# One transfer of weights and one of keys change places in GpSimd's order of issue

## The chip, the cores and the metric

The kernel runs on one core of one Trainium2 chip. The time is that of the device for one execution, in microseconds. A core has five engines that run side by side, each with its own order of instructions: TensorE (PE; PEld is its weight load), VectorE (DVE), ScalarE (ACT), GpSimd (POOL) and SyncE (SP). Transfers between memory and the chip are issued by SyncE, GpSimd and, at the start, ScalarE, and are carried by 16 DMA engines. In the profile, q0 is the queue of transfers that GpSimd issues and q1 that of SyncE's.

## What is computed

Causal attention for 4 batches, 8 heads, 768 positions and head size 64, in which five of the heads see only 4 sink positions and a window of 64, followed by a gated feed-forward layer over the 3072 resulting rows:

```python
scores = q @ k^T / sqrt(64)                    # per batch and head
scores = where(mask, scores, -1e9)             # heads 0, 2, 6: causal; the others: causal and (sink or window)
x = softmax(scores) @ v                        # laid out as [3072, 512]
h = x @ w_in                                   # w_in  [512, 2048]
g = h * sigmoid(beta * h)
out = g @ w_out                                # w_out [2048, 512], out [3072, 512] f32
```

Inputs and output are float32; the kernel multiplies in bf16.

## The kernel before

The work is cut into eight chunks: a batch and a half of its positions (384 rows). They go two batches at a time, first halves ahead of second halves, so the third and fourth chunks (numbers 2 and 3) are the second halves of batches 0 and 1. A chunk has four units, each a pair of heads; unit 12 is the first of the fourth chunk. For a unit TensorE makes the scores (line 482), ScalarE their exponentials, VectorE or the added masks remove what is not seen, and TensorE multiplies with the values (line 563). For a chunk that is done, TensorE makes h in 16 groups (line 631), ScalarE and VectorE make g of it (lines 636 and 639), and TensorE makes three output tiles of 128 rows from the 16 pieces of g, in four parts of four products (line 684): the first part takes the first quarter of w_out, the fourth part the last. ScalarE copies an output tile out of its bank (line 688), and SyncE stores it (line 690).

Every engine's order is written out by hand. The string RAMP, a list of words that `do` carries out one by one, orders the first eight units; PLAN orders the rest, with `later` for steps that come due after a time of a planner's clock. The words that matter here:

- `wi0` to `wi3`: GpSimd issues one quarter of w_in (line 141); `wo0` to `wo3`: one quarter of w_out (line 145). Both turn float32 into bf16 on the way.
- `ro3`: GpSimd issues the next row load of the fourth chunk (`load_rows`, line 284). There are twelve: six of keys, then six of queries, each 128 rows of four heads, turned into bf16. They go into tile `s`.
- `dk3`, `dq3`: SyncE transposes the fourth chunk's keys into KT (line 300) and its queries into QTD (line 303), three transfers each; one needs two row loads.
- `vo1`, `vo2`, ...: GpSimd copies the values of a chunk's windows and sinks into VO (lines 261 and 262).

In the order of RAMP the transfers that GpSimd issues are, counted from one: the four of w_in (1 to 4), `wo0`, `wo1`, `wo2` (5 to 7), `ro3` (8), `wo3` (9), and the other eleven `ro3` (10 to 20), after which those of the fifth chunk follow. All wait their turn in one queue. Between them GpSimd has copies and casts to do, in its one order. `ro` and `wo` add nothing to the planner's clock.

The quarter of w_out is loaded, and a row load issued, by

```python
nc.gpsimd.dma_start(out=w_out_sb[:, f, :], in_=moe_w_out.rearrange("(fo fi) d -> fi fo d", fi=128)[:, f, :])
...
nc.gpsimd.dma_start(out=ROWS[c % 2, name][:, t, i * 4 * D:(i + 1) * 4 * D].rearrange("p (h d) -> p h d", d=D),
                    in_=src[b, i:H:2, r:r + 128, :].rearrange("h p d -> p h d"))
```

Of the kernel before, what the change touches and what calls it, by code (L numbers as in the profile page):

```python
# [18 lines left out]
def kernel(  # L19
# [792 lines left out]
    def feed(x):  # L812
# [20 lines left out]
        ex3.0 qk4.1 tk5 ad4.0 ex3.1 tq5 pv3 pv3 pv3 cx0a kk6v no2 qk4.0 tk7 ex4.1 kq5a kk5v no3 ko5 ex4.0 qk5.0 ko6  # L833
        kk7v wi1 tq6 xx1 ex5.0 ko7 qk5.1 ex5.1 tq7 kq6v ad6.0 kq7v cv1.0a cx1v wi2 qk6.0 wi3 ad6.1 ml1 qk6.1 ex6.0
        ex6.1 hm mm cv1.1g ma5.v mlg cv1.2g pv4 rk hf mm ad7.0 qk7.0 vo1 wo0 wo1 pv5 ma5.1 pv4 lq2.1g wo2 pv4 lv3.0g
        no4 ad7.1 qk7.1 lv3.1 ex7.0 pv5 rq pv7 pv5 pv6 pv7 no5 pv6 ro3 wo3 pv6 ex7.1 pv7 ml1 mm lv3.2 no7 no6 xx2
        ro3 cx2a mA mA xx3 ro3 cx3v mm mm mA mA mm mm ro3 mA mm mA mm mm mm mA cq8g mm mA mm ck8g mA mm mm mA mA mm
        ro3 mm mm ro3 mA mA mb mb tt8 mb mb mb
    """
# [114 lines left out]
```

## Time and profile before

| | us |
|---|---|
| median of 3 runs | 229.96 |
| the runs | 229.87 to 230.05 |
| the profiled execution | 230.6 |
| its span, first to last instruction | 228.9 |

The profile is of one execution. Its span is 1.7 us shorter than that execution's time. TensorE is busy for 97% of it, at a granted clock of 0.998 of full speed; ScalarE for 67%, VectorE for 61%, GpSimd for 38%. A row of the order of time gives start, duration, engine, line and operation, the tile written and the tile read, and in brackets the idle time ahead of it with what ended it. "DMA to landing" is the time from the start of the issuing instruction to the landing of its data.

### The profile page before, as it was taken

The numbers are of one execution on the slowest core, as the hardware profiler recorded it, in microseconds if no ns is written. First come the engines' busy times: TensorE is split into PE (matmuls) and PEld (weight loads), VectorE is DVE, ScalarE is ACT, GpSimd is POOL, SyncE is SP. The second block draws the span as 40 slices with busy tenths as digits, with TensorE's granted clock in tenths as the row PEclk, the third lists the DMA queues.
The fourth block names the chain that finished last, engine by engine and source line by source line (L and its number), as shares of the span: only waits on it lengthen the run. The fifth ranks groups of instructions, "written<-read, shape, count | busy, mean of one in ns | idle before, by whom it ended". The sixth has DMA issues, their size and how long they took to land.

```text
span 228.9 us, 5039 instructions
## 1 busy us (share of the span) xinstructions
PE 221.7 (97%) x1919; PEld 126.9 (55%) x1919; DVE 139.5 (61%) x343; ACT 153.6 (67%) x252; POOL 87.3 (38%) x144
## 2 busy tenths in 40 slices
PE   8999999979999999999999999999999999999993
PEld 3566666634555665555654565556645665456553
DVE  2578888852485679436942589566863779028600
ACT  2589788826867799348944797669876877138521
POOL 6467934168245369444039308960430000000000
PEclk9999999999999999999999999999999999999999
DMA  6999999999999799979779998799803030111012
GB/s 201 246 307 223 213 229 197 192 225 171 152 193 131 164 157 155 121 181 153 100 149 124 147 174 134 106 161 137 195 4 105 25 80 0 49 54 38 0 49 93
DMA packets 95384, 31.67 MB, mean 138 GB/s; under 512 B 81776, under 2 KB 92416, under 8 KB 95360
## 3 DMA queue, kind: packets, MB, share of 16 engines
q1 hardware_dynamic: 58880, 22.82, 49.2%
q0 software_dynamic: 35904, 8.13, 44.6%
q10 hardware_dynamic: 576, 0.40, 0.6%
q8 instruction: 15, 0.25, 0.5%
q14 instruction: 9, 0.07, 0.1%
HBM read 27.27 MB, written 6.29 MB: 147 GB/s over the span
## 4 chain that ended last, share of the span: by engine, by line
PE 76%; DMA 16%; POOL 3%; DVE 1%; ACT 1%; SPq 1%; issue 0%; ACTq 0%; POOLq 0%
PE mm L684 34%; PE mm L631 18%; DMA w_out_sb<-in_moe_w_out_dram 10%; PE sp L631 8%; PE sp L482 6%; PE po L563 6%; DMA vs<-in_v_dram 4%; DMA s<-in_q_dram 2%; PE mm L669 2%; POOL w_out_sb L145 1%; PE mm L353 1%; PE po L544 1%; PE mm L482 1%; DVE es L515 1%; POOL VX L253 1%; SPq L133 1%
## 5 line engine op out<-in xcount | busy, mean ns | idle before, releaser
L684 PE MATMUL mm<-w_out_sb,gT 128*128 128x512 bf16 x368 | 86.0, 379 | 1.4 <-DMA w_out_sb<-in_moe_w_out_dram 1.4
L491 ACT ACTIVATE es<-sp 128x768 bf16<-128x768 f32 (+2 forms) x72 | 56.5, 834 | 18.8 <-PE sp L482 18.5
L631 PEld LDWEIGHTS <-w_in_sb 128*128 128x128 bf16 x512 | 47.7, 98 | 30.1 <-issue 0.6
L631 PE MATMUL mm<-xT,w_in_sb 128*128 128x384 bf16 x340 | 63.3, 326 | 0.2 <-DVE gT L639 0.2
L684 PEld LDWEIGHTS <-gT 128*128 128x128 bf16 x368 | 33.4, 98 | 37.5 <-issue 3.1
L636 ACT ACTIVATE th<-mm,beta_h 128x384 f32<-128x384 f32 x85 | 48.4, 586 | 6.5 <-PE mm L631 1.8
L639 DVE SCALAR_TENSOR_TENSOR gT<-th,mm 128x384 bf16<-128x384 f32 x85 | 45.6, 550 | 7.1 <-ACT th L636 3.8
L631 PE MATMUL sp<-xT,w_in_sb 128*128 128x384 bf16 x172 | 33.6, 326 | 0.0
L688 ACT ACTIVATE osb<-mm 128x512 f32<-128x512 f32 x23 | 13.9, 602 | 27.1 <-PE mm L684 26.7
L563 PEld LDWEIGHTS <-es 128*128 128x128 bf16 x472 | 22.8, 98 | 11.9 <-issue 1.1
L253 POOL CAST VX<-vs 128x512 bf16<-128x512 f32 x15 | 9.5, 633 | 51.2 <-DMA vs<-in_v_dram 48.4
L639 DVE SCALAR_TENSOR_TENSOR gT<-th,sp 128x384 bf16<-128x384 f32 x43 | 23.3, 551 | 5.9 <-ACT th L636 3.7
L636 ACT ACTIVATE th<-sp,beta_h 128x384 f32<-128x384 f32 x43 | 24.8, 583 | 2.4 <-PE sp L631 0.2
L284 POOL DMA_DIRECT2D s<-in_k_dram x30 | 22.4, 758 | 9.4 <-DMA w_in_sb<-in_moe_w_in_dram 4.7
L563 PE MATMUL po<-VX,es 128*128 128x65 bf16 x360 | 24.7, 194 | 0.0
L284 POOL DMA_DIRECT2D s<-in_q_dram x30 | 22.5, 781 | 3.6 <-DMA w_out_sb<-in_moe_w_out_dram 2.7
L572 DVE RECIPROCAL rec<-po 128x6 f32<-128x6 f32 x28 | 5.4, 193 | 28.0 <-PE po L563 27.8
L482 PE MATMUL sp<-QTD,KT 64*128 64x128 bf16 (+2 forms) x258 | 19.2, 240 | 0.0
L509 DVE TENSOR_TENSOR es<-es,Mh 128x768 bf16<-128x768 bf16 (+1 forms) x26 | 14.8, 595 | 5.0 <-ACT es L491 4.4
L576 DVE TENSOR_TENSOR x<-po,rec 128x384 bf16<-128x384 f32 x28 | 15.6, 557 | 1.0
L482 PEld LDWEIGHTS <-KT 64*128 64x128 bf16 x278 | 11.0, 94 | 5.5 <-issue 3.7
L261 POOL COPY VO<-VX 128x512 bf16<-128x512 bf16 x16 | 10.0, 644 | 9.5 <-DVE VX L253 9.5
(75 smaller groups left out, 160.2 us busy)
## 6 DMA issues: line engine op xcount, KB each, us to landing
vs<-in_v_dram SPq DMA_DIRECT2D x24, 256.0 KB, 4.8
out_dram<-osb SPq DMA_DIRECT2D x23, 256.0 KB, 2.6
w_in_sb<-in_moe_w_in_dram POOLq DMA_DIRECT2D x4, 512.0 KB, 9.8
w_out_sb<-in_moe_w_out_dram POOLq DMA_DIRECT2D x4, 512.0 KB, 17.0
s<-in_k_dram POOLq DMA_DIRECT2D x30, 64.0 KB, 4.7
s<-in_q_dram POOLq DMA_DIRECT2D x30, 64.0 KB, 5.5
s<-in_k_dram SPq DMA_DIRECT2D x4, 384.0 KB, 8.7
s<-in_q_dram SPq DMA_DIRECT2D x4, 384.0 KB, 9.6
```

The costliest lines, as they stand in the source:

```text
L253: copy(out=VX[b % 2][:, h2 * HT + t, :, 0:D], in_=staged["v", c][:, t])
L284: nc.gpsimd.dma_start(out=ROWS[c % 2, name][:, t, i * 4 * D:(i + 1) * 4 * D].rearrange("p (h d) -> p h d", d=D), in_=src[b, i:H:2, r:r + 1 ...
L482: nc.tensor.matmul(sps[i][r][:, x * 128:y * 128], key(a, lhs), s["QT"][half(a), qi * 128:(qi + y - x) * 128], start=first, stop=first or y ...
L491: nc.scalar.activation(out=views[i].rearrange("p r k j -> p r (k j)"), in_=banks[2][:, :, 0:n * 128], func=ACTF.Exp, scale=scale)
L509: eng.tensor_mul(ev[:, :, 0:n], ev[:, :, 0:n], Mh[h2][:, None, m0:m0 + n].to_broadcast([128, 2, n, 128]))
L563: nc.tensor.matmul(po[:, qi, hh, :], e, val, start=(j == 0), stop=(j == len(lst) - 1))
L576: nc.vector.tensor_mul(xg[g][:, :, :, u % 2, :].rearrange("p a t d -> p t a d"), po[:, :, :, 0:D], rec.to_broadcast([128, HT, 2, D]))
L631: nc.tensor.matmul(hp[:, 0:HALF], w_in_sb[:, mo, fi * 128:(fi + 1) * 128], xT[c][:, mo, :], start=(mo == 0), stop=(mo == MO - 1))
L636: nc.scalar.activation(out=th, in_=hp[:, 0:HALF], func=ACTF.Tanh, scale=beta_h[:, fi:fi + 1])
L639: nc.vector.scalar_tensor_tensor(out=gTs[c][:, fi, :], in0=th, scalar=1.0, in1=hp[:, 0:HALF], op0=ALU.add, op1=ALU.mult)
L684: nc.tensor.matmul(op, gTs[c][:, fi, ns * 128:(ns + 1) * 128], w_out_sb[:, fi, :], start=(fi == 0), stop=(fi == FO - 1))
L688: nc.scalar.activation(out=osb, in_=op, func=ACTF.Copy, scale=0.5)
```

## The change

In RAMP the words `ro3 wo3` become `wo3 ro3`: GpSimd issues the last quarter of w_out as its eighth transfer and the fourth chunk's first row load of keys as its ninth. The other words, and all that the words do, stay as they are.

```diff
-        no4 ad7.1 qk7.1 lv3.1 ex7.0 pv5 rq pv7 pv5 pv6 pv7 no5 pv6 ro3 wo3 pv6 ex7.1 pv7 ml1 mm lv3.2 no7 no6 xx2
+        no4 ad7.1 qk7.1 lv3.1 ex7.0 pv5 rq pv7 pv5 pv6 pv7 no5 pv6 wo3 ro3 pv6 ex7.1 pv7 ml1 mm lv3.2 no7 no6 xx2
```

## The prediction

> **What bounds the kernel now.** I read the page first: the engines' busy time, then the chain that ended last, and then the order of time on TensorE and on GpSimd around the one place of that chain that is not TensorE's own work.
>
> ```profile
> span 228.9 us, 5039 instructions
> PE 221.7 (97%) x1919; PEld 126.9 (55%) x1919; DVE 139.5 (61%) x343; ACT 153.6 (67%) x252; POOL 87.3 (38%) x144
> ```
>
> TensorE has work for 221.7 of 228.9 us. A change pays, then, only where it shortens one of the few gaps on TensorE, or costs where it opens one. The chain of waits, from 28 us on, has this:
>
> ```profile
> 28.52 22.11 DMA w_out_sb<-in_moe_w_out_dram
> 50.67 3.61 PE mm L684 x16
> ```
>
> The chain runs through the transfer of w_out's last quarter: issued at 28.52, landed 22.11 us later, at 50.63, and the products of line 684 start 0.04 us behind it. After 50.67 the chain goes through TensorE, with a few stretches of ScalarE and VectorE, to the end. The order of time on TensorE shows how long it stood there:
>
> ```profile
> 48.28 1.03 PE L684 MATMUL mm<-w_out_sb,gT 128*128 128x512 bf16 x4
> 50.67 3.61 PE L684 MATMUL mm<-w_out_sb,gT 128*128 128x512 bf16 x16 [1.36 <-DMA w_out_sb<-in_moe_w_out_dram]
> ```
>
> The first twelve products of an output tile need quarters 0 to 2; the thirteenth needs quarter 3. TensorE was ready at 48.28 + 1.03 = 49.31 and idle for 1.36 us. This is the gap that the change bears on, and 1.36 us is the most that can be had from it directly.
>
> **What the change moves.** Two GpSimd instructions change places. The order of time on GpSimd (the idle time and its releaser stand in brackets):
>
> ```profile
> 27.02 0.76 POOL L145 DMA_DIRECT2D w_out_sb<-in_moe_w_out_dram  x1
> 27.79 0.77 POOL L284 DMA_DIRECT2D s<-in_k_dram  x1
> 28.52 0.78 POOL L145 DMA_DIRECT2D w_out_sb<-in_moe_w_out_dram  x1
> 29.25 0.79 POOL L284 DMA_DIRECT2D s<-in_k_dram  x1
> 31.59 0.74 POOL L284 DMA_DIRECT2D s<-in_k_dram  x1 [1.54 <-DMA w_in_sb<-in_moe_w_in_dram]
> ...
> 45.59 0.74 POOL L284 DMA_DIRECT2D s<-in_q_dram  x1 [2.66 <-DMA w_out_sb<-in_moe_w_out_dram]
> 46.93 0.74 POOL L284 DMA_DIRECT2D s<-in_q_dram  x1 [0.59 <-DMA s<-in_k_dram]
> 47.66 0.62 POOL L261 COPY VO<-VX 128x512 bf16<-128x512 bf16 x1
> 49.88 1.17 POOL L261 COPY VO<-VX 128x512 bf16<-128x512 bf16 x2 [1.59 <-DVE VX L253]
> 51.11 1.46 POOL L262 COPY VO<-VX 4x1536 bf16<-4x1536 bf16 x1
> 52.52 2.22 POOL L284 DMA_DIRECT2D s<-in_q_dram  x3
> 55.12 0.84 POOL L284 DMA_DIRECT2D s<-in_q_dram  x1 [0.37 <-DMA s<-in_k_dram]
> 56.41 0.74 POOL L284 DMA_DIRECT2D s<-in_k_dram  x1 [0.46 <-DMA s<-in_k_dram]
> ```
>
> The quarter's issue moves from 28.52 to 27.79, and the row load's from 27.79 to 28.57 (27.79 + 0.78). No instruction is added or taken away, and the 0.77 and 0.78 us of issue only trade places. The 0.73 us of earlier issue are not the gain: both transfers wait a long time in the queue behind others. What counts is where each stands in it, and for this I asked for single transfers' times from issue to landing (the last number of the pairs below; the first fence has the second and third quarters, of which the later, at 27.02, took 18.3).
>
> ```profile
> L145 POOL DMA_DIRECT2D w_out_sb<-in_moe_w_out_dram x2: 747/754/760, 26.2 to 27.0; - x2
> DMA to landing us min/median/max: 15.7/17.0/18.3
> ```
> ```profile
> L284 POOL DMA_DIRECT2D s<-in_k_dram x1: 770/770/770, 27.8 to 27.8; - x1
> DMA to landing us min/median/max: 18.9/18.9/18.9
> ```
> ```profile
> L145 POOL DMA_DIRECT2D w_out_sb<-in_moe_w_out_dram x1: 780/780/780, 28.5 to 28.5; - x1
> DMA to landing us min/median/max: 22.1/22.1/22.1
> ```
> ```profile
> L284 POOL DMA_DIRECT2D s<-in_k_dram x1: 790/790/790, 29.3 to 29.3; - x1
> DMA to landing us min/median/max: 23.1/23.1/23.1
> ```
>
> Issue plus duration gives the landings: third quarter 27.02 + 18.3 = 45.32; row load 27.79 + 18.9 = 46.69; last quarter 28.52 + 22.1 = 50.62; second row load 29.25 + 23.1 = 52.35. They land in the order of issue, 1.37, 3.93 and 1.73 us apart. So the GpSimd queue is being worked off in order and without a pause, and a row load holds it for about 1.4 to 1.7 us.
>
> **The sum.** Take the row load out from in front of the last quarter. The quarter then lands 3.93 us behind the third one, at 45.32 + 3.93 = 49.25, which is 1.37 us sooner. TensorE is ready at 49.31 and would find it there, or nearly: with the 0.04 us from landing to start of the chain, 49.29. The gap of 1.36 us goes to about 0. The bounds: a row load is worth nothing if it runs in the shadow of other transfers, and 1.73 us by the second row load's spacing, but the gap caps this at 1.36. So the direct gain lies between 0 and 1.36. I take 1.3, since the spacing of 1.37 was measured for this very transfer, at this very place, and a tenth may be lost where the two mixes of packets differ.
>
> Why should the row load have a cost of its own, at an eighth of the quarter's size (the page's list of issues: count, KB each, median us to landing)?
>
> ```profile
> w_out_sb<-in_moe_w_out_dram POOLq DMA_DIRECT2D x4, 512.0 KB, 17.0
> s<-in_k_dram POOLq DMA_DIRECT2D x30, 64.0 KB, 4.7
> ```
>
> The answer of the DMA view for 41.99 to 45.35 us, ahead of the third quarter's landing (queue, packets, MB, share of 16 engines):
>
> ```profile
> q1 hardware_dynamic: 819, 0.23, 47.6%
> q0 software_dynamic: 817, 0.40, 86.5%
> ```
>
> The GpSimd queue (q0) and SyncE's (q1) moved equally many packets, 817 and 819, though 0.40 against 0.23 MB: they take turns by packets, so a load of many small packets costs as many turns as one of large ones. The Trainium skill, "DMA: Bandwidth & Descriptors", section "Queues, rings and completion order", says that each engine goes round the queues that have work and changes over at packet borders; the counts here agree with it. By that rule the bytes of the load do not matter and its turns do. By bytes alone, 64 of 512 KB, the row load would be worth 3.93 / 8 = 0.49 us, and the gain with it.
>
> **What the swap does to others.** The first row load now comes behind the quarter. By the same spacings it lands where the quarter did, at about 50.6, and the second at 52.35 as before. The transposes of the fourth chunk's keys need both, so nothing is later for them.
>
> A wait changes its content, though. GpSimd's row loads at 31.59, 45.59 and 46.93 each wait for the transfer issued eight places earlier: 31.59 is the eleventh of the queue and waits for a piece of w_in, the third; 45.59, the fifteenth, starts 0.27 us behind the third quarter's landing (45.32), the seventh; 46.93, the sixteenth, 0.24 us behind the row load's (46.69), the eighth. With the change, the eighth is w_out's last quarter, landing at 49.25. So the row load of 46.93 starts at about 49.5, some 2.6 us later, and behind it in GpSimd's order stand the three copies of VO, line 262's copy and four more row loads. Counted on: issue to 50.2, the copies to 52.0 (0.62 + 1.17; their own wait on VectorE ended by 49.88), line 262 to 53.5, three row loads to 55.7 where they ended at 54.74, the next to 56.5, and the first row load of the chunk after at 56.5 instead of 56.41. The slip is 2.6 us at first, about 1 us behind the copies, and 0.1 us at the end, because the short waits that stood at 49.88, 55.12 and 56.41 take it up.
>
> Two covers hide it. One is the queue's backlog:
>
> ```profile
> L284 POOL DMA_DIRECT2D s<-in_q_dram x1: 740/740/740, 46.9 to 46.9; - x1
> DMA to landing us min/median/max: 11.8/11.8/11.8
> ```
> ```profile
> L284 POOL DMA_DIRECT2D s<-in_q_dram x1: 740/740/740, 52.5 to 52.5; - x1
> DMA to landing us min/median/max: 7.5/7.5/7.5
> ```
>
> The load of 46.93 landed at 58.7 and the next, issued at 52.5, at 60.0, right behind it. Issued at 49.5 and 53.5 they still have over 6 us of queue ahead of them. The other is the distance to who needs the result:
>
> ```profile
> 64.73 0.19 PE L563 MATMUL po<-VO,es 128*128 128x65 bf16 x1
> ```
> ```profile
> L303 SPq DMA_TRANSPOSE QTD<-s x1: 1190/1190/1190, 65.1 to 65.1; - x1
> DMA to landing us min/median/max: 3.2/3.2/3.2
> ```
> ```profile
> 71.73 0.61 PE L482 MATMUL sp<-QTD,KT 64*128 64x384 bf16 x8
> ```
>
> The VO copies end at 53.5, and the first product with VO comes at 64.73, or 63.4 if TensorE gains 1.3: ten us to spare. The fourth chunk's queries are transposed last at 65.1 and landed at 68.3; their first scores stand at 71.73, or 70.4 with the gain: 2.1 us to spare. This is the thinnest cover. If it were gone, each us of lateness would cost one.
>
> So the sum is -1.3 + 0 + 0. The profiled execution took 230.6 us with a span of 228.9, so it would be 229.3 with a span of 227.6. The median of the runs was 229.96, 0.64 below the profiled one; I take the same 1.3 off: 228.7.
>
> **Rivals.** First, no change: the last quarter lands at 50.6 wherever its issue stands, since the landing is that of the slowest of 16 engines and these were saturated. For it: the long 3.93 us spacing may be that of a straggling engine, which the row load's few packets would not have held up. Against it: the landings in order and the 1.37 us between third quarter and row load. The time would be 230.0. The Trainium skill, same page, "Two DMAs through the same engine are not ordered", says that nothing orders transfers across the 16 engines, which would speak for this; the four landings here came in order all the same. Chance 0.12.
>
> Second, slower: the changed wait. The sixteenth transfer now waits for a long one instead of a short one, and the queries behind it come late. It decides when the queries' last transposes land after 70.4 instead of 68.3, and it takes the whole gain once they land after 71.73, 3.4 us late. If the backlog hid none of it and the loads lost one more place, of a quarter's 3.93 us, the landing would be 72.2: a gap of 0.5 us over the old course, 230.5; with the 2.6 us of the wait on top, 74.8 and 233.1. For it: GpSimd's order is strict and the wait is sure to come. Against: the 6 us of backlog. Chance 0.14.
>
> Third, a part of the gain given back: TensorE comes 1.3 us sooner to something that does not move with it. The queries (2.1 us to spare after the gain) are the nearest that I found; most others, the stores and the x transposes, are issued by work that follows TensorE. Keeping half gives 229.3, still faster. By bytes alone (0.49 us) the time would be 229.5, at the border of faster. Both are inside the faster case, except for the last tenth. That the change does not do what it says I hold out at under 0.01: the two words issue one transfer each and advance no planner clock.
>
> **How the numbers follow.** A measurement of this kernel can tell about 0.2%, 0.46 us, from no change, so "same" runs from 229.50 to 230.42. Faster 0.74: full gain (0.62) and partial gain (0.12). Same 0.12. Slower 0.14. The full gain's own range is 228.4 to 229.0. The predicted time is its middle, 228.7. The range goes from 228.3, the whole 1.36 with 0.3 of other shifts, to 230.2, which takes in the partial gain and most of no change, and leaves out the slower case.
>
> **What would show it.** Right: the idle time in front of line 684's sixteen products falls from 1.36 to under 0.2 us; the last quarter's landing is near 49.3; the row load that waited for keys at 46.93 waits for w_out and starts near 49.5; the first VO product and the scores at 71.73 come about 1.3 us sooner, with no new wait for QTD; the span is 227.6. Wrong: a landing still at 50.6 (first rival), or a gap on TensorE before 70 to 75 us that ends with a transposed load of queries or with VO (second), or a gap later that ends with a transfer (third).

## The result, and the profile after

The changed kernel takes 228.61 us (median of 6 runs, 228.36 to 229.09) against 229.92 for the kernel before beside it. The ratio is 0.9947, with a 95% interval of 0.9934 to 0.9960: faster by 1.31 us. A second set of runs gave 228.43 us and 0.9938 (0.9926 to 0.9950). The forecast was 228.7.

The page of the changed kernel, span and busy time:

```profile
span 226.8 us, 5040 instructions
PE 221.3 (98%) x1919; PEld 126.9 (56%) x1919; DVE 140.1 (62%) x343; ACT 153.4 (68%) x252; POOL 86.9 (38%) x144
```

The spans differ by 2.1 us, more than the medians. The profiled execution of before, 230.6 us, was 0.64 above its median, that of the changed kernel, 228.58, stood at its own. The medians carry the result; the traces tell where it comes from.

TensorE's order of time at the place of the gap:

```profile
47.68 0.50 PE L353 MATMUL mm<-idb,qkb 128*128 128x128 bf16 x6
48.01 4.48 PE L684 MATMUL mm<-w_out_sb,gT 128*128 128x512 bf16 x20
52.33 0.50 PE L353 MATMUL mm<-idb,qkb 128*128 128x128 bf16 x6
```

Where before four products, 1.36 us of idle time and sixteen products stood, there are twenty without a pause. They take 4.48 us, where the four and the sixteen took 1.03 + 3.61 = 4.64 without the idle time: in an unbroken row the products overlap a little, so the break itself cost another 0.16 us. The transfers, each with its time from issue to landing (second and third quarter; last quarter; first and second row load):

```profile
L145 POOL DMA_DIRECT2D w_out_sb<-in_moe_w_out_dram x2: 750/756/762, 26.2 to 27.0; - x2
DMA to landing us min/median/max: 15.3/16.6/17.9
```
```profile
L145 POOL DMA_DIRECT2D w_out_sb<-in_moe_w_out_dram x1: 770/770/770, 27.8 to 27.8; - x1
DMA to landing us min/median/max: 20.6/20.6/20.6
```
```profile
L284 POOL DMA_DIRECT2D s<-in_k_dram x2: 777/781/785, 28.6 to 29.3; - x2
DMA to landing us min/median/max: 21.7/22.2/22.7
```

With the starts from GpSimd's order (27.05, 27.82, 28.55, 29.33) they land at 44.95, 48.42, 50.25 and 52.0; times to landing are given to 0.1 us, and the differences below are good to about that. The last quarter comes 3.47 us behind the third, where it was 5.30 before; the row load between them was worth 1.83 us. TensorE was ready at 48.01 + 1.03 = 49.04, so the quarter was there 0.62 us ahead of its use. Only 1.36 of the 1.83 us could be had.

GpSimd's order of time shows the wait that changed its content:

```profile
45.20 0.74 POOL L284 DMA_DIRECT2D s<-in_q_dram  x1 [2.64 <-DMA w_out_sb<-in_moe_w_out_dram]
48.70 0.81 POOL L284 DMA_DIRECT2D s<-in_q_dram  x1 [2.77 <-DMA w_out_sb<-in_moe_w_out_dram]
49.51 0.63 POOL L261 COPY VO<-VX 128x512 bf16<-128x512 bf16 x1
50.48 1.18 POOL L261 COPY VO<-VX 128x512 bf16<-128x512 bf16 x2 [0.35 <-DVE VX L253]
51.72 1.46 POOL L262 COPY VO<-VX 4x1536 bf16<-4x1536 bf16 x1
53.14 2.98 POOL L284 DMA_DIRECT2D s<-in_q_dram  x4
```

The row load that started at 46.93 behind a row load now starts at 48.70, 0.28 us behind the last quarter's landing. Its wait is 2.77 us instead of 0.59, and the VO copies end at 53.2 instead of 52.6. Nobody pays: the first product with VO, the queries' last transpose and the scores that use it stand at

```profile
62.94 0.19 PE L563 MATMUL po<-VO,es 128*128 128x65 bf16 x1
69.94 0.61 PE L482 MATMUL sp<-QTD,KT 64*128 64x384 bf16 x8
```
```profile
L303 SPq DMA_TRANSPOSE QTD<-s x2: 1189/1198/1206, 61.8 to 63.2; - x2
DMA to landing us min/median/max: 3.0/3.4/3.9
```

Both products come 1.79 us sooner than before (64.73 and 71.73), and neither waits. The queries' last transpose is issued at 63.2 and has landed by 67.1 at the latest, at least 2.8 us ahead of its use. Before, it was issued at 65.1: the queries came sooner, though their loads were issued later. The row load issued at 48.70 instead of 46.93 landed at 58.5 instead of 58.7, and the last one, issued at 55.4 instead of 55.1, at 63.1 instead of 65.0, in both kernels 0.1 us ahead of that transpose. So the queue's backlog took up the whole lateness; why it cleared even sooner than before, no run takes apart.

### The profile page after: what moved, and what is told of

It reads as the page before. It is cut to its first block, busy times and chain, and to the rows that moved or that the text cites. A ratio compares the mean times of both kernels' runs of the same rounds, so it can differ in the third digit from the quotient of the medians.

```text
span 226.8 us, 5040 instructions
## 1 busy us (share of the span) xinstructions
PE 221.3 (98%) x1919; PEld 126.9 (56%) x1919; DVE 140.1 (62%) x343; ACT 153.4 (68%) x252; POOL 86.9 (38%) x144
## 3 DMA queue, kind: packets, MB, share of 16 engines
q0 software_dynamic: 35904, 8.13, 41.9%
## 4 chain that ended last, share of the span: by engine, by line
PE 92%; DMA 4%; DVE 1%; POOL 1%; issue 0%; ACT 0%; ACTq 0%
PE mm L684 36%; PE mm L631 25%; PE sp L631 12%; PE po L563 6%; PE sp L482 6%; DMA w_in_sb<-in_moe_w_in_dram 4%; PE po L544 2%; PE mm L669 2%; PE mm L170 1%; PE mm L353 1%; PE mm L482 1%; PE mm L601 1%; PE sp L453 0%; PE mm L563 0%; POOL VO L261 0%; POOL VO L262 0%
## 5 line engine op out<-in xcount | busy, mean ns | idle before, releaser
L631 PE MATMUL mm<-xT,w_in_sb 128*128 128x384 bf16 x340 | 63.2, 326 | 0.3 <-DMA w_in_sb<-in_moe_w_in_dram 0.3
```

What stands on the lines that cost most here:

```text
L631: nc.tensor.matmul(hp[:, 0:HALF], w_in_sb[:, mo, fi * 128:(fi + 1) * 128], xT[c][:, mo, :], start=(mo == 0), stop=(mo == MO - 1))
```

## The experiments

**A second row load ahead of the quarter.** This is the order of before, with one more step in the wrong direction.

```diff
- pv6 ro3 wo3 pv6 ...            ro3 cx2a mA mA
+ pv6 ro3 ro3 wo3 pv6 ...        cx2a mA mA
```

> The order of before, with a second row load of keys ahead of w_out's last quarter (ro3 ro3 wo3). Theory (place in the queue): the quarter lands one row load later than before, 1.4 to 1.8 us, at 52.0 to 52.4 in a profile; TensorE's gap ahead of line 684's thirteenth product grows from 1.36 to about 3.0 us; time 229.9 + 1.6 = 231.5 us (231.2 to 231.8). Rival (the landing does not depend on the order): gap 1.4 us, 229.9 us.

It took 231.39 us (231.29 to 231.57), 1.0069 of before (1.0056 to 1.0081). The second and third quarter, the two row loads and the last quarter of its profile, and TensorE's row behind the gap:

```profile
L145 POOL DMA_DIRECT2D w_out_sb<-in_moe_w_out_dram x2: 747/754/760, 25.9 to 26.7; - x2
DMA to landing us min/median/max: 15.4/16.7/18.0
```
```profile
L284 POOL DMA_DIRECT2D s<-in_k_dram x2: 770/775/780, 27.5 to 28.2; - x2
DMA to landing us min/median/max: 18.6/19.1/19.7
```
```profile
L145 POOL DMA_DIRECT2D w_out_sb<-in_moe_w_out_dram x1: 787/787/787, 28.9 to 28.9; - x1
DMA to landing us min/median/max: 22.7/22.7/22.7
```
```profile
51.72 3.61 PE L684 MATMUL mm<-w_out_sb,gT 128*128 128x512 bf16 x16 [2.88 <-DMA w_out_sb<-in_moe_w_out_dram]
```

The quarter lands at 28.95 + 22.7 = 51.65, 6.94 us behind the third (26.71 + 18.0 = 44.71). With none, one and two row loads in front the distance is 3.47, 5.30 and 6.94 us, and TensorE's gap 0, 1.36 and 2.88. The extra 1.52 us of gap shows as 1.47 in the median. The first rival, that the landing does not follow the order, is out.

**The same bytes in fewer packets.** The order of before, with the one row load ahead of the quarter replaced by 64 KB in rows of 512 B. The page counts 35520 packets on the GpSimd queue instead of 35904: 384 fewer, which is 128 instead of 512 for this load. The load takes other keys, so a part of the fourth chunk's keys is wrong in this run; it reads them from one unbroken stretch of memory where the narrow load reads four, and the run does not tell this apart from the number of packets. (Lines from 288 on are shifted by four.)

```diff
+ if c == 3 and name == "k" and t == 0 and i == 0:
+     nc.gpsimd.dma_start(out=ROWS[1, "k"][:, 0, 0:4 * D],
+                         in_=src[b, 0, 0:512, :].rearrange("(p x) d -> p (x d)", x=4))
+     return
```

> The order of before, but the one row load ahead of w_out's last quarter brings the same 64 KB as 128 packets of 512 B instead of 512 of 128 B (it takes other keys, so that part of the fourth chunk's keys is wrong). Theory (turns by packets set a load's price): the load costs a quarter of its 1.8 us, some 0.5 us; the last quarter lands 3.5 + 0.5 us behind the third, at about 49.2; the gap goes from 1.36 to 0 to 0.2 us; 228.6 to 228.9 us. Rival (bytes set the price): the last quarter lands 5.3 us behind the third as in before, gap 1.4 us, 229.9 us.

It took 228.79 us (228.38 to 229.18), 0.9959 of before (0.9946 to 0.9972). Third quarter, wide load and last quarter, and TensorE:

```profile
L145 POOL DMA_DIRECT2D w_out_sb<-in_moe_w_out_dram x1: 762/762/762, 26.8 to 26.8; - x1
DMA to landing us min/median/max: 17.8/17.8/17.8
```
```profile
L284 POOL DMA_DIRECT2D s<-in_k_dram x1: 571/571/571, 27.5 to 27.5; - x1
DMA to landing us min/median/max: 17.7/17.7/17.7
```
```profile
L145 POOL DMA_DIRECT2D w_out_sb<-in_moe_w_out_dram x1: 777/777/777, 28.1 to 28.1; - x1
DMA to landing us min/median/max: 20.7/20.7/20.7
```
```profile
47.94 4.53 PE L688 MATMUL mm<-w_out_sb,gT 128*128 128x512 bf16 x20
```

The quarter lands 4.21 us behind the third (28.06 + 20.7 less 26.75 + 17.8), so the wide load costs 4.21 - 3.47 = 0.74 us where the narrow one of the same size cost 1.83. The number of packets is the larger part of a load's price here, though not the whole: a quarter of 1.83 would be 0.46, and one packet of 512 B cost 0.74 / 128 = 5.8 ns where one of 128 B cost 1.83 / 512 = 3.6. With 0.74 the quarter just arrives in time (48.76, TensorE ready at 48.97), and the gap is gone without the swap. That the two queues take turns by packets shows in this case beyond the one stretch of the prediction: from 46.7 to 50.5 us of the changed kernel the GpSimd queue moved 1108 packets and SyncE's 1110, though 0.16 against 0.74 MB. The Trainium skill's rule of turns by packets ("DMA: Bandwidth & Descriptors", "Queues, rings and completion order") agrees with this in direction. By that section a packet holds several descriptors; whether the packets that the profile counts are these, no run here shows.

**The long wait taken out of the VO copies' way.** The changed kernel, with the waiting row load issued behind those copies (the words for the queries' loads stand in PLAN).

```diff
- ro3 ro3 ck9v b cq9a dk3 b cv2.1v cv2.0v vo2 T ro3
+ ro3 ck9v b cq9a dk3 b cv2.1v cv2.0v vo2 ro3 T ro3
```

> The changed kernel, with the row load of queries that waits for w_out's last quarter (at 48.70 in its profile) put behind the second chunk of VO copies, so that GpSimd's copies no longer stand behind that wait. Theory (the changed wait is hidden): the VO copies end about 1 to 1.5 us sooner, TensorE does not move, 228.6 us as the changed kernel, within 0.3. Rival (the changed wait eats part of the gain): 0.3 to 1 us faster than the changed kernel, 227.6 to 228.3 us.

It took 228.33 us (228.16 to 229.09), 0.9942 of before (0.9927 to 0.9956). GpSimd's copies then stand at

```profile
45.64 0.62 POOL L261 COPY VO<-VX 128x512 bf16<-128x512 bf16 x1
49.32 1.18 POOL L261 COPY VO<-VX 128x512 bf16<-128x512 bf16 x2 [3.05 <-DVE VX L253]
50.56 1.46 POOL L262 COPY VO<-VX 4x1536 bf16<-4x1536 bf16 x1
```

and end at 52.0, 1.2 us sooner, where they wait for VectorE instead. TensorE has no wait more or less at this place. Its ratio lies between the changed kernel's two (0.9947 and 0.9938) and cannot be told from them: the changed wait costs nothing that these runs, with intervals of about 0.3 us to either side, can measure.

**GpSimd held up by 3.8 us.** The changed kernel, with memsets of an unused tile behind the row load at 48.70. (From here on, lines are shifted by one: 510 is 509, 564 is 563.)

```diff
+ hd: for x in range(n): nc.gpsimd.memset(scratch, 0.0)      # scratch: 128 x 512 bf16
- ro3 ro3 ck9v b
+ ro3 ro3 hd6 ck9v b
```

> The changed kernel with six memsets of a tile that nobody reads (about 0.5 us each, 3 us in all) on GpSimd behind that same row load of queries: the VO copies and the last four row loads of queries come some 3 us later. Theory (3.7 us lie between the landing of the queries' last transpose, 66.2, and their first scores, 69.9, and the queue still has work when the loads are issued): no gap on TensorE, 228.6 us as the changed kernel, within 0.3. Rival (the cover of the queries is thin, and lateness at GpSimd costs TensorE): 1 to 3 us slower, 229.6 to 231.6 us.

It took 229.07 us (228.49 to 229.46), 0.9963 of before (0.9949 to 0.9977): above the changed kernel by 0.46 us, with intervals that overlap. The time is between the theory's and the rival's, and the reason is neither's. GpSimd, VectorE and TensorE of this run:

```profile
56.51 3.05 POOL L285 DMA_DIRECT2D s<-in_q_dram  x4
...
60.27 1.54 POOL L262 COPY VO<-VX 128x512 bf16<-128x512 bf16 x2
```
```profile
60.45 1.76 DVE L510 TENSOR_TENSOR es<-es,Mh 128x768 bf16<-128x768 bf16 x2
```
```profile
63.23 0.20 PE L564 MATMUL po<-VO,es 128*128 128x65 bf16 x1 [0.39 <-DVE x L577]
```

and of VectorE, then of GpSimd, in the changed kernel:

```profile
60.72 1.07 DVE L509 TENSOR_TENSOR es<-es,Mh 128x768 bf16<-128x768 bf16 x2
```
```profile
59.35 0.62 POOL L261 COPY VO<-VX 128x512 bf16<-128x512 bf16 x1 [1.87 <-DVE VX L253]
```

The gap of 0.39 us ends with VectorE, not with a transfer. The two mask multiplies took 1.76 instead of 1.07 us while GpSimd copied beside them. The queries came no later: their last load was issued at 58.7 instead of 55.4 and landed at 63.1 in both, and their last transpose was issued at 63.3, against 63.2.

```profile
L304 SPq DMA_TRANSPOSE QTD<-s x2: 1189/1197/1205, 62.0 to 63.3; - x2
DMA to landing us min/median/max: 2.5/2.8/3.0
```

My reading of where the cover is thin was wrong, so the next run puts the same hold behind all queries.

**The same hold, ahead of the fourth chunk's VO copies.**

```diff
- ck11a ro4 a b
+ ck11a ro4 hd6 a b
```

> The changed kernel with the six memsets (3.8 us in hold_3) behind all row loads of queries, just ahead of the fourth chunk's VO copies on GpSimd: no query comes later, but two VO copies come at about 60.7 us, beside VectorE's two mask multiplies at 60.72. Theory (hold_3 lost its 0.39 us on TensorE because GpSimd's VO copies ran beside VectorE's mask multiplies, which took 1.76 instead of 1.07 us, and not for late queries): the two multiplies take 1.6 to 1.8 us here too, TensorE waits 0.3 to 0.4 us ahead of the first VO product at about 63, 229.0 us. The Trainium skill, SBUF — State Buffer, section Who interferes with whom, has a VectorE instruction in a two-port mode and GpSimd exclude each other. Rival (late queries cost it): multiplies at 1.07 us, no gap, 228.6 us.

It took 229.10 us (228.69 to 229.95), 0.9964 of before (0.9951 to 0.9977), against 0.9938 (0.9926 to 0.9950) for the changed kernel run beside it:

> The changed kernel once more, beside the runs of this set. Theory and rival alike: 228.6 us, within 0.3. It serves as the base for the two holds, and for the comparison with no_long_wait's 228.33 us.

That took 228.43 us (228.28 to 228.72). The rows of the hold: GpSimd, VectorE and TensorE.

```profile
56.81 3.75 POOL L802 MEMSET scratch<- 128x512 bf16 x6
60.51 1.49 POOL L262 COPY VO<-VX 128x512 bf16<-128x512 bf16 x2
```
```profile
58.60 0.75 DVE L249 CAST qkb<-s 128x384 bf16<-128x384 f32 x1
59.27 0.82 DVE L254 CAST VX<-vs 128x512 bf16<-128x512 f32 x1
...
60.73 1.68 DVE L510 TENSOR_TENSOR es<-es,Mh 128x768 bf16<-128x768 bf16 x2
```
```profile
63.42 0.20 PE L564 MATMUL po<-VO,es 128*128 128x65 bf16 x1 [0.31 <-DVE x L577]
```

No query is late here: their last transpose was issued at 63.1. The same multiplies take 1.68 us and the same gap opens, 0.31 us. So hold_3's gap came from VectorE and GpSimd working side by side. The median lost 0.67 us to the changed kernel beside it and 0.49 to its first set (228.61). TensorE's rows show about as much: the first VO product stands at 63.42 here and at 62.94 in the changed kernel's first profile, with the products ahead of it at the same time (62.08) in both. Of these 0.48 us, 0.31 are the gap and 0.17 the overlap lost by the break.

**GpSimd held up by 11 us.** hold_3 with eighteen memsets (`hd18`), to find where lateness does reach TensorE.

> hold_3 with eighteen memsets instead of six, about 11.3 us on GpSimd: the VO copies of the third chunk end near 64.1 us, 1.2 us behind their first use at 62.9, and the last row load of queries is issued near 67, against 55.4 in the changed kernel. Theory (GpSimd's lateness costs only from there): a gap of about 1.2 us ahead of the first VO product and one of 1 to 2 us ahead of unit 12's scores (69.9 in the changed kernel), which end with VO and with transposed queries; 230.5 to 232 us. Rival (the queue and the order leave still more room): under 229.5 us.

It took 232.78 us (231.49 to 234.04), 1.0128 of before (1.0093 to 1.0164), above what was expected. The profiled execution took 233.55. TensorE's waits in it, and the stretches of time behind them (busy times of TensorE, its loads, VectorE, ScalarE and GpSimd, granted clock, DMA share, GB/s):

```profile
PE sp L483 <- DMA QTD<-s: 1.9, 1, 1.9
PE po L564 <- POOL VO L263: 1.5, 1, 1.5
```
```profile
74.00:76.00 2.00, 1.80 (x10) 0.92 (x10) 0.00 (x0) 1.65 (x2) 1.31 (x2) 0.50 1.35 265
76.00:78.00 2.00, 2.00 (x17) 0.92 (x16) 0.20 (x1) 0.00 (x0) 0.00 (x0) 0.67 1.88 134
```

Both expected gaps are there and end with VO and with transposed queries, as the second rival of the prediction described it. The hold of 11 us made the last transpose of queries 7.5 us late (70.7 instead of 63.2), where the hold of 3.8 us in hold_3 made it 0.1 late; how much between the two the cover bears was not tried. Most of the rest of the loss in this execution is the granted clock, 0.50 and 0.67 of full speed in the 4 us behind the second gap, which the trace has as one stretch of 3.41 us at 0.50, from 73.89 to 77.30: 2 x 0.50 + 2 x 0.33 = 1.7 us, with the gaps 5.1 of the 5.0 by which the span of this run (231.8) exceeds the changed kernel's. The other executions have no trace. Their mean clocks, 0.991 to 1.000, do not follow their times (231.8 us at 0.992, 232.02 at 1.000), so the clock alone does not account for the scatter between them.

## Why the prediction was right

**The gap.** It was to go from 1.36 us to under 0.2, and is 0. Its step by step: the landing was put at 49.25 and was 48.42. Of the 0.83 us, 0.37 are the third quarter's own earlier landing (44.95 instead of 45.32, no doing of the change), and 0.46 the row load's price, 1.83 us instead of the 1.37 that I took from the distance between two landings. This is the term of the sum that was mis-sized. The distance ahead of the load's landing is too short a measure: behind it, the last quarter then took 3.93 us, and without the load 3.47, so 0.46 of the load's price fell there. Why part of it falls behind the landing is not shown. The distance with and without the load is the right measure, and two_ahead gave 1.64 for a further load. The error did not matter, as the gap caps what can be had. The reason for the price, packets and not bytes, held: wide_rows took the gap away with the same bytes, and the 0.49 us that the prediction gave by bytes alone is not what the narrow load cost.

**The gain kept.** 1.3 of 1.36 us was forecast to reach the end; 1.31 did. That the number came within 0.1 us is in part luck: the intervals are about 0.3 us to either side, the second set gave 1.49, and the tenth that the prediction took off for other mixes of packets was not lost. The trace shows the first VO product and unit 12's scores 1.79 us sooner. Of this, 0.27 were there already at the first products of line 684 (45.95 instead of 46.22), where the quarter is not yet needed; 1.36 are the gap and 0.16 the overlap regained with it. Most of what the spans differ beyond 1.79 stands at one place: before, TensorE waited 0.18 us at 87.40 for VectorE, and the changed kernel has no such wait. Whether that belongs to the change is not shown.

**The changed wait.** GpSimd's row load was put at 49.5 and came at 48.70, with the landing; the VO copies' end at 53.5, and was 53.2. That this is hidden was right, and no_long_wait shows it. The cover by the queue's backlog was right too: the loads issued later landed no later.

**The thinnest cover.** Here the step failed. I named the queries, with 2.1 us to spare, as the next to be late. hold_3 made their loads 3.4 us later (56.51 instead of 53.14) and their last transpose no later, because the backlog I counted on was even better than counted: the last load, issued 3.3 us later, landed at the same 63.1. What does come first when GpSimd slips is a collision with VectorE: two copies beside two multiplies, 0.6 to 0.7 us on VectorE and 0.3 to 0.4 of idle time on TensorE. The prediction looked at who waits for GpSimd and not at who works beside it. In the changed kernel itself the copy is out of the way: it runs from 59.35 to 59.97, and the multiplies start at 60.72.

**The rivals.** The first (landing independent of the order) is refuted by two_ahead. The second exists, as hold_18 shows, but far from here. For the third, a part given back, nothing was seen: TensorE's waits in the changed kernel all stand ahead of 22 us.

## What to carry to other kernels

Read the wait of the bound engine for a transfer back to the queue: what stands in front of that transfer, and how far its landing moves with and without it. A load of many small packets in front of an urgent one can cost far more than its share of the bytes: here an eighth of the quarter's size cost 1.83 us, about half of the quarter's own 3.47. Here either putting it behind or making its packets larger removed the wait. Moving an issue also changes which transfer a later issue waits for, here eight places on; count that wait out to whoever stands behind it, and ask as well which engine will then work beside the late one.

## What the runs showed of the hardware

- The price of one 64 KB load in a queue while a second queue is busy beside it: 1.83 us as 512 packets, 0.74 as 128. The two queues moved equally many packets, 817 and 819 or 1108 and 1110, whatever their size.
- All 68 transfers that GpSimd issued landed in the order of their issue in each of the nine profiles.
- VectorE's multiplies of two tiles and GpSimd's copies slow each other: 1.07 to 1.68 and 1.76 us for two multiplies. The Trainium skill, "SBUF — State Buffer", section "Who interferes with whom", says that a VectorE instruction with two inputs in SBUF and a GpSimd instruction that reads SBUF contend for a shared port; the runs agree. The expectation of hold_at_vo3 named that section's rule for two-port modes, which by the same section these multiplies do not have. GpSimd's memsets, which only write, slowed VectorE's casts from float32: the two casts of hold_at_vo3 took 0.75 and 0.82 us, and three of four such casts in hold_18 0.76 to 0.83, where the changed kernel has

```profile
58.60 0.35 DVE L248 CAST qkb<-s 128x384 bf16<-128x384 f32 x1
58.87 0.42 DVE L253 CAST VX<-vs 128x512 bf16<-128x512 f32 x1
```

- The granted clock fell to 0.50 for 3.41 us behind two gaps of 1.54 and 1.91 us within 10 us (hold_18); in the 3.41 us ahead of the drop TensorE was busy for 1.50. Behind the single gap of 2.88 us in two_ahead it stayed at 1.00. What sets it off was not tried.
